# Half of a second matrix product in seven block products instead of eight, on one Trainium2 core

## The chip, the cores and the metric

The kernel runs on one core of one Trainium2 chip. The metric is the device time of one execution in microseconds; lower is better. Every run of the kernel before agrees with the others within 0.25%.

## What is computed

The inputs are 8 batches of 576 tokens, 8 heads of 64. A packed attention (32 packed queries a head) is followed by a mixer and a two-layer network with residual:

```
p_packed = sm_attn(p, k, v)                    # per head, 32 rows
x  = sm_attn(q, p_packed, p_packed)            # [B, 576, 8*64] after a transpose
h  = x^T @ U @ V                               # rank 32, along the tokens
u  = x + h^T
ch = relu(u @ w_ch1) @ w_ch2                   # 512 -> 2048 -> 512
out = u + ch
```

All of it is float32 in and out. The matrix products of the network run in fp32r with each operand split in a high and a low part, so that one product takes three passes (high x high, high x low, low x high).

## The kernel before

**Layout.** A batch has 576 = 9 x 64 tokens. Eight of the nine make four tiles of 128 tokens; the ninth, 64 tokens a batch, is called LAST. The hidden size 2048 is cut in 16 blocks `kt` of 128. The network's two products are called GEMM 1 (to hidden, L749) and GEMM 2 (back to 512 columns, L780).

**Opening.** A list of words (`opening`, L154) sets the order of everything up to batch 0: it loads and converts the weights, computes the packed attention of all batches, and runs attention and most of the network of batch 0. The weights of GEMM 2 stay in SBUF as `w2h` and `w2l` for the whole kernel, and w1 as four tiles `w1t`. For each batch w1 is multiplied by that batch's packed rows (`fold`, L536 to L560), which gives `wth` and `wtl`, the weights that GEMM 1 uses.

**Steady state.** From batch 1 on a loop (L923) runs, for each `kt`: GEMM 1 of this block (`gemm1`, 12 matmuls: 6 of 320 columns for row half 0, which holds the ninth tokens, and 6 of 256 for row half 1), one or two steps of the attention of the next batch (`steps`), and GEMM 2 of the block before (`gemm2`: four token tiles, three matmuls of 512 columns each, into four PSUM banks `o`). After a row half of GEMM 1 ScalarE writes relu as the high part `hh`, ScalarE keeps the ninth tokens in `hj`, and VectorE writes the low part `hl` straight from PSUM (L758 to L770). Every fourth block one `fold` follows. The residual u reaches `o` as small matmuls (`add_u`, L791) from tiles that `get` (L721) has brought back from HBM. At the end of a batch `store` (L797) copies the four banks out.

**Ninth tokens.** Two batches' LAST tokens make one tile of 128. After every second batch `joint` (L819) runs GEMM 2 for it, 48 matmuls of 512 columns, with parts split by `joint_parts` (L807), and `store_joint` (L835) writes it. The last batch's joint product is the program's last matmul work.

**What sets the order.** In the opening and in the loop the program's order is the order in which each engine gets its instructions; nothing is rescheduled. An engine that waits holds everything behind it. Nearly all DMAs are issued by SP's queue in program order.

Of the kernel before, what the change touches and what calls it, by code (L numbers as in the profile page):

```python
# [20 lines left out]
def packed_attention_mixer_kernel(  # L21
# [114 lines left out]
    w1t = [pipe.tile([P, DF], F32, name=f"w1t{x}", tag=f"w1t{x}") for x in range(4)]  # L136
# [191 lines left out]
    def attention(b, res):  # L328
# [92 lines left out]
        def put():  # L421
            for g in range(2):
                nc.sync.dma_start(out=aD[b][g * P:g * P + P], in_=st["aT", g])
            nc.sync.dma_start(out=ppD[b].rearrange("(g p) d -> p g d", g=2), in_=ppall[:, b])
# [20 lines left out]
        if b < 2:  # L445
# [90 lines left out]

    def fold_products(b, c):
        f_ps = [bank() for _ in range(2)]
        for h in range(H):
            g, z = h // 4, h % 2  # L540
            xs, zs = slice(32 * (h % 4 ^ g), 32 * (h % 4 ^ g) + 32), slice(64 * z, 64 * z + 64)
            nc.tensor.matmul(f_ps[g][xs], lhsT=ppT[b][zs, g, xs], rhs=w1t[h // 2][zs, QW * c:QW * c + QW],  # L542
                             start=True, stop=True)
        return f_ps
# [156 lines left out]
    def close_sA():  # L701
        actx.close()
        sB = pools["B"] = ctx.enter_context(tc.tile_pool(name="sB", bufs=2, reuse_waits="tile"))
        kept["hj"] = sB.tile([P, NK + 1, P], F32, name="hj", bufs=1)
        kept["aP"] = sB.tile([P, H, P], F32, name="aP", bufs=1)
# [9 lines left out]
    def jslot(b, kt):  # L715
        return NK if kt == 0 and (b // 2) % 2 else kt


    aL, ppP = {}, {}

    def get(b):  # L721
        sB, aP = pools["B"], kept["aP"]
        aL[b] = sB.tile([32, H, I], F32, name="aL", bufs=2)
        ppP[b] = sB.tile([P, H, D], F32, name="ppP", bufs=2)
        a, y = (x.rearrange("(h n) x -> n h x", n=32) for x in (aD[b], ppD[b]))
        for t in range(4):
            ts_ = slice(32 * t, 32 * t + 32)
            nc.sync.dma_start(out=aP[ts_], in_=a[:, :, cols(t)])
            nc.sync.dma_start(out=ppP[b][ts_], in_=y)
        nc.sync.dma_start(out=aL[b], in_=a[:, :, LAST])  # L730
# [10 lines left out]
    class Batch:  # L741
        def __init__(self, b):
            self.b = b
            self.ah, self.al = res[b]
            self.js = slice(I * (b % 2), I * (b % 2) + I)
            self.h, self.p = {}, {}
            self.o = None

        def half1(self, kt, r):  # L749
            c, kq = divmod(kt, 2)  # L750
            wh, wl = wt[self.b, c]
            ks, ns = slice(kq * P, kq * P + P), HALF[r]
            h_ps = self.p[kt, r] = psT.tile([P, 512], F32, name="h_ps", tag="k")
            for g in range(2):
                mm3(h_ps[:, :ns.stop - ns.start], (wh[:, g, ks], wl[:, g, ks]),
                    (self.ah[:, g, ns], self.al[:, g, ns]), g == 0, g == 1)

        def high1(self, kt, r):  # L758
            if kt not in self.h:
                self.h[kt] = tuple(pools["B"].tile([P, SM], F32R, name=f"h{x}", tag=f"h{x}", bufs=2) for x in "hl")  # L760
            nc.scalar.activation(self.h[kt][0][:, 4 * I * r:4 * I * r + 4 * I], self.p[kt, r][:, :4 * I], AF.Relu)  # L761

        def last1(self, kt):
            nc.scalar.activation(kept["hj"][:, jslot(self.b, kt), self.js], self.p[kt, 0][:, LAST], AF.Relu)  # L764
# [26 lines left out]
        def add_u(self):  # L791

            for h, t in product(range(H), range(4)):
                ts_ = slice(32 * t, 32 * t + 32)
                nc.tensor.matmul(self.o[t][:, place(h)], lhsT=kept["aP"][ts_, h], rhs=ppP[self.b][ts_, h], start=False, stop=False)  # L795

        def store(self):  # L797
            for j in range(2):
                os_ = bits_tile().bitcast(F32).rearrange("p x t -> p (x t)").rearrange("p (a x) -> p a x", a=2)
                nc.scalar.copy(os_[:, 0], self.o[2 * j])  # L800
                nc.vector.tensor_copy(os_[:, 1], self.o[2 * j + 1])
                for a in range(2):
                    c0 = j + 2 * a
                    nc.sync.dma_start(
                        out=out[self.b].rearrange("(i c) m -> i c m", c=NT)[:, c0:c0 + 5:4], in_=os_[:, a])

    def joint_parts(b, n):  # L807

        hi, lo = conv_tile(F32R), conv_tile(F32R)
        k0 = 4 * n  # L810
        for (dst, src) in ((slice(0, 1), jslot(b, k0)), (slice(1, 4), k0 + 1)):
            w = dst.stop - dst.start
            src = kept["hj"][:, src:src + w].rearrange("p k x -> p (k x)")
            cs = slice(P * dst.start, P * dst.stop)
            nc.scalar.copy(hi[:, cs], src)
            nc.vector.tensor_tensor(lo[:, cs], src, hi[:, cs].bitcast(F32), op=ALU.subtract)
        return hi, lo

    def joint(b, parts):  # L819

        oj = pools["O"].tile([P, DM], F32, name="o", tag="o")
        for kt in range(NK):
            if kt % 4 == 0:
                hi, lo = parts.pop(0)
                if kt // 4 + 2 < NK // 4:
                    parts.append(joint_parts(b, kt // 4 + 2))
            cs = slice(P * (kt % 4), P * (kt % 4) + P)
            mm3(oj, (hi[:, cs], lo[:, cs]), w2_parts(kt), kt == 0, kt == NK - 1)
            if kt == 0:
                for h, i in product(range(H), range(2)):  # L830
                    nc.tensor.matmul(oj[I * i:I * i + I, place(h)], lhsT=aL[b - 1 + i][:, h], rhs=ppP[b - 1 + i][:32, h],
                                     start=False, stop=False)
        return oj

    def store_joint(b, oj):  # L835
        os_ = conv_tile(F32)
        n = DM // 2
        nc.scalar.copy(os_[:, :n], oj[:, :n])
        nc.vector.tensor_copy(os_[:, n:], oj[:, n:])
        for i, queue in enumerate((nc.sync, nc.scalar)):  # L840
            queue.dma_start(out=out[b - 1 + i].rearrange("(i c) m -> c i m", c=NT)[8], in_=os_[I * i:I * i + I])
# [80 lines left out]
    last, parts = kept["cur"], []  # L922
    for b in range(1, B):  # L923
        now = Batch(b)
        oj = None
        ahead = attention(b + 2, res) if b + 2 < B else []
        for kt in range(NK):
            now.gemm1(kt)
            if oj and kt == 1:
                store_joint(b - 1, oj)  # L930
            if steps and (b < 2 or kt % 4 != 2) and (b, kt) != (1, 0):
                steps.pop(0)()
            if kt > 0:
                now.gemm2(kt - 1)
            else:
                last.gemm2(NK - 1)
                last.store()
                if last.b % 2 == 1:
                    oj = joint(last.b, parts)
            if kt % 4 == 2 and (b, kt) != (B - 1, NK - 2):  # L940
                n = b * NPC + kt // 4 + 1
                fold(n // NPC, n % NPC)
            if kt == 6:
# [47 lines left out]
```

## Time and profile before

| | |
|---|---|
| median of 3 runs | 805.23 us (804.2 to 806.06) |
| profiled execution | 805.29 us |
| its span in the profile | 803.5 us |
| mean granted TensorE clock | 0.998 |
| HBM read, written | 53.64 MB, 15.60 MB |
| DMA queue of SP | 27.6% of 16 engines' time |

The difference of 1.8 us between the execution and its span lies outside of what the profiler shows. The page cuts the span in 40 slices of 20.1 us; a digit is the busy share in tenths:

```profile
PE   8999999999999999999999999999999999999997
DVE  4898789843443234333334233333434233332231
ACT  4788645543233232333234232333234232332221
PEclk9999999999999999999999999999999999999999
DMA  9999984460004200230012200230022200030001
```

PE is TensorE, DVE VectorE, ACT ScalarE, POOL GpSimd; "PEld" in other views is TensorE's weight load, which overlaps the matmuls. The opening takes the first eight slices, where VectorE and ScalarE are busy too. Behind it only TensorE is full.

### The profile page before, as it was taken

Reading aid. Unit: us, or ns where it says so; the run is one execution under the profiler, and the core shown is the slowest. Engines: PE = TensorE matmul, PEld = TensorE weight load, DVE = VectorE, ACT = ScalarE, POOL = GpSimd, SP = SyncE. Lnnn points to the kernel's source line nnn. Section 1 sums busy time; section 2 is a strip of 40 time slices with the busy share of each in tenths; the row PEclk is TensorE's granted clock in tenths of the full one; section 3 lists DMA queues with packets and bytes.
Section 4 is the critical chain, followed back from the end, with each engine's and each line's share of the span. In section 5 each row is a group of like instructions: output and inputs, shape, how many; then the busy total and the mean of one; then the engine's idle time right before and its main releaser. Section 6 shows DMA issues by size and latency. Waiting matters only on the chain.

```text
span 803.5 us, 15400 instructions
## 1 busy us (share of the span) xinstructions
PE 790.7 (98%) x6272; PEld 640.6 (80%) x6272; DVE 361.1 (45%) x797; ACT 307.7 (38%) x879; POOL 79.3 (10%) x109
## 2 busy tenths in 40 slices
PE   8999999999999999999999999999999999999997
PEld 6667778788888788878888788888887788878886
DVE  4898789843443234333334233333434233332231
ACT  4788645543233232333234232333234232332221
POOL 1023021101110011101100011101100011100000
PEclk9999999999999999999999999999999999999999
DMA  9999984460004200230012200230022200030001
GB/s 323 335 354 296 302 195 138 131 195 1 1 1 151 57 1 2 81 113 2 1 66 86 56 1 2 81 114 1 1 66 86 56 2 1 16 113 1 1 1 65
DMA packets 59285, 70.22 MB, mean 87 GB/s; under 512 B 20816, under 2 KB 40272, under 8 KB 59216
## 3 DMA queue, kind: packets, MB, share of 16 engines
q1 hardware_dynamic: 58896, 68.73, 27.6%
q8 instruction: 49, 0.80, 0.4%
q10 hardware_dynamic: 320, 0.52, 0.2%
q14 instruction: 20, 0.16, 0.1%
HBM read 53.64 MB, written 15.60 MB: 86 GB/s over the span
## 4 chain that ended last, share of the span: by engine, by line
PE 88%; DMA 4%; DVE 4%; ACT 3%; issue 1%; POOL 0%; SPq 0%; ACTq 0%; DVEq 0%
PE o L95 16%; PE o L97 16%; PE o L96 16%; PE h_ps L95 9%; PE h_ps L97 8%; PE h_ps L96 8%; PE t_ps L542 4%; DMA bits<-in_moe_w_ch_dram 3%; PE o L795 2%; PE t_ps L297 1%; DMA kx<-in_k_dram 1%; PE t_ps L317 1%; PE t_ps L323 1%; PE t_ps L408 1%; PE m_ps L669 1%
## 5 line engine op out<-in xcount | busy, mean ns | idle before, releaser
L95 PE MATMUL o<-w2h,hh 128*128 128x512 f32 x512 | 205.0, 400 | 0.0
L97 PE MATMUL o<-w2h,hl 128*128 128x512 f32 x512 | 201.9, 394 | 0.3 <-DVE hl L769 0.3
L96 PE MATMUL o<-w2l,hh 128*128 128x512 f32 x512 | 201.2, 393 | 0.0
L769 DVE SCALAR_TENSOR_TENSOR hl<-h_ps,hh 128x256 fp32r<-128x256 f32 x256 | 106.4, 422 | 197.3 <-ACT hj L764 179.5
L761 ACT ACTIVATE hh<-h_ps 128x256 fp32r<-128x256 f32 x256 | 98.4, 386 | 180.7 <-PE h_ps L97 168.9
L95 PE MATMUL h_ps<-ah,wth 128*128 128x320 f32 (+1 forms) x512 | 158.0, 309 | 0.2 <-ACT hj L764 0.2
L96 PE MATMUL h_ps<-al,wth 128*128 128x320 f32 (+1 forms) x512 | 150.8, 295 | 0.0
L97 PE MATMUL h_ps<-ah,wtl 128*128 128x320 f32 (+1 forms) x512 | 150.7, 294 | 0.0
L95 PEld LDWEIGHTS h_ps<-ah,wth 128*128 128x128 f32 x512 | 96.3, 188 | 25.9 <-issue 20.2
L97 PEld LDWEIGHTS o<-w2h,hl 128*128 128x128 f32 x512 | 96.2, 188 | 22.4 <-DVE hl L769 0.7
L95 PEld LDWEIGHTS o<-w2h,hh 128*128 128x128 f32 x512 | 96.5, 189 | 21.1 <-issue 4.9
L96 PEld LDWEIGHTS o<-w2l,hh 128*128 128x128 f32 x512 | 96.5, 188 | 16.4
L96 PEld LDWEIGHTS h_ps<-al,wth 128*128 128x128 f32 x512 | 96.3, 188 | 2.2
L97 PEld LDWEIGHTS h_ps<-ah,wtl 128*128 128x128 f32 x512 | 96.6, 189 | 0.0
L555 DVE TENSOR_TENSOR wtl<-t_ps,wth 128x256 fp32r<-128x256 f32 x128 | 48.5, 418 | 95.0 <-ACT wth L553 92.0
L553 ACT CAST wth<-t_ps 128x256 fp32r<-128x256 f32 x128 | 43.4, 375 | 100.5 <-PE t_ps L542 94.0
L440 POOL TENSOR_TENSOR al<-aT,ah 128x320 fp32r<-128x320 f32 (+1 forms) x32 | 27.6, 866 | 223.9 <-ACT ah L436 195.8
L364 POOL TENSOR_TENSOR e<-e,m 128x576 f32<-128x576 f32 x16 | 19.0, 1186 | 272.7 <-DVE m L360 272.7
L542 PE MATMUL t_ps<-w1t,ppT 64*32 64x512 f32 x512 | 34.8, 601 | 0.0
L306 ACT COPY xT<-t_ps 128x512 f32<-128x512 f32 x30 | 17.6, 586 | 38.8 <-PE t_ps L297 38.1
L764 ACT ACTIVATE hj<-h_ps 128x64 f32<-128x64 f32 x128 | 28.2, 220 | 2.0 <-PE h_ps L97 1.1
L364 POOL TENSOR_TENSOR e<-e,s 128x576 f32<-128x576 f32 x16 | 19.3, 1207 | 93.7 <-DVE s L376 77.9
(125 smaller groups left out, 806.0 us busy)
## 6 DMA issues: line engine op xcount, KB each, us to landing
bits<-in_moe_w_ch_dram SPq DMA_DIRECT2D x32, 512.0 KB, 4.5
kx<-in_k_dram SPq DMA_DIRECT2D x16, 576.0 KB, 6.3
x<-in_q_dram SPq DMA_DIRECT2D x16, 576.0 KB, 5.0
vt<-in_v_dram SPq DMA_DIRECT2D x32, 256.0 KB, 6.0
out_dram<-bits SPq DMA_DIRECT2D x32, 256.0 KB, 2.4
aD<-aT SPq DMA_DIRECT2D x16, 288.0 KB, 2.2
aP<-aD SPq DMA_DIRECT2D x32, 128.0 KB, 3.3
ppP<-ppD SPq DMA_DIRECT2D x32, 64.0 KB, 3.0
```

Of the source, the lines that this page charges most:

```text
L95: nc.tensor.matmul(ps, lhsT=lh, rhs=rh, start=start, stop=False)
L96: nc.tensor.matmul(ps, lhsT=lh, rhs=rl, start=False, stop=False)
L97: nc.tensor.matmul(ps, lhsT=ll, rhs=rh, start=False, stop=stop)
L306: copy(scalar)(t[:, 2 * h:2 * h + 2, :4 * I].rearrange("p z (k y) -> p z k y", k=2), src)
L364: nc.gpsimd.tensor_tensor(e, e, st[what, g].unsqueeze(2).to_broadcast([P, S // 32, 32]), op=op)
L440: nc.gpsimd.tensor_tensor(al[:, g, ns], aT[:, ns], ah[:, g, ns].bitcast(F32), op=ALU.subtract)
L542: nc.tensor.matmul(f_ps[g][xs], lhsT=ppT[b][zs, g, xs], rhs=w1t[h // 2][zs, QW * c:QW * c + QW], start=True, stop=True)
L553: nc.scalar.copy(hi[:, g], src)
L555: nc.vector.tensor_tensor(lo[:, g], src, hi[:, g].bitcast(F32), op=ALU.subtract)
L761: nc.scalar.activation(self.h[kt][0][:, 4 * I * r:4 * I * r + 4 * I], self.p[kt, r][:, :4 * I], AF.Relu)
L764: nc.scalar.activation(kept["hj"][:, jslot(self.b, kt), self.js], self.p[kt, 0][:, LAST], AF.Relu)
L769: nc.vector.scalar_tensor_tensor(hl[:, ms], self.p[kt, r][:, :4 * I], 0.0, hh[:, ms].bitcast(F32), op0=ALU.max, op1=ALU.subtract)
```

## The change

Batches 0 and 1 run as before. From batch 2 on GEMM 2 is done differently.

**Sweeps.** A batch's 512 tokens are taken in two sweeps of 256 tokens (2 x 128), r = 0 and 1. A sweep goes over the hidden size in 8 pairs of blocks, c = 0 to 7. With the two token tiles, the two hidden blocks of a pair and the two halves of 256 output columns, a pair is a 2 x 2 by 2 x 2 block product. For even c (`PAIRS`) it is made by Strassen's method in Winograd's form: 7 block products of three 256-column matmuls. For odd c the plain 8 block products are made. All of them accumulate in four PSUM banks per sweep (8 half banks, 7 of them Strassen terms), which are combined once, at the end of the sweep.

**Ninth tokens.** The LAST tokens of four batches (256 rows) make one more sweep after batches 3 and 7, in place of a joint product after each second batch. `save_last` writes each batch's ninth tokens to HBM (`hjD`).

**Operands.** VectorE makes the sums of the weights once, in the last blocks of batch 1 (`begin_sums`, `make_sums`, `split_sums`); they go over three of the four `w1t` tiles, so w1 is kept in HBM (`w1D`) and brought back in pieces of 1 MB (`stream_w1`) ahead of each fold. The sums of the activations are made per pair (`sums`, VectorE), and high and low parts are split from SBUF (`split_high` ScalarE, `split_low` VectorE), no longer from PSUM. GEMM 1 of row half 1 is computed in sweep 0 for c < 5 and its result written to HBM (`hold_out`, `hD`), and read back in sweep 1 (`load`).

**Order.** The loop of batches 2 to 7 is replaced by lists of words, as in the opening: `prologue`, `batch_steps` and, where a joint sweep follows, `joint_steps`.

```diff
+    def begin_sums(c):
...
+        nc.vector.tensor_tensor(x.rearrange("p (k n) -> p k n", k=2), h, l, op=ALU.add)
...
+    def make_sums(c):
...
+        vec(t[:, 0:2], x[:, 0:4:3], x[:, 1:2].to_broadcast([P, 2, HW_]), op=ALU.subtract)
+        vec(t[:, 2], t[:, 0], x[:, 3], op=ALU.add)
+        vec(t[:, 3], x[:, 2], t[:, 2], op=ALU.subtract)
...
+    def split_sums(c):
...
+        parts = [(h1, l1)] + [(room[:, i, 0], room[:, i, 1]) for room in rooms]
+        for k, (h, l) in enumerate(parts):
+            nc.scalar.copy(h, t[:, k])
+            nc.vector.tensor_tensor(l, t[:, k], h.bitcast(F32), op=ALU.subtract)
...
+    def stream_w1(c):
+        t = w1t["s"] = pipe.tile([P, 4, QW], F32, name="w1s", tag=f"w1t{NPC - 1}", bufs=1)
+        nc.sync.dma_start(out=t.rearrange("p x n -> p (x n)"), in_=w1D[c])
...
+    class Sweep:
+        def load(self, c):
+            src = hD[self.now.b][P * c:P * c + P] if self.r else hjD[self.q].rearrange("p (c x) -> p c x", c=8)[:, c]
+            l = self.l[c] = sums_tile()
+            nc.sync.dma_start(out=l[:, :4].rearrange("p k n -> p (k n)"), in_=src)
...
+        def leave(self, c, i):
...
+            nc.scalar.activation(dst[:, 256 * (i % 2):256 * (i % 2) + 256], src, AF.Relu)
...
+        def sums(self, c):
+            l, vec = self.l[c], nc.vector.tensor_tensor
+            vec(l[:, 4:6], l[:, 1:3], l[:, 0:1].to_broadcast([P, 2, P]), op=ALU.add)
+            vec(l[:, 6], l[:, 2], l[:, 4], op=ALU.add)
+            vec(l[:, 7], l[:, 3], l[:, 6], op=ALU.add)
+        def split_high(self, c):
+            t = pools["B"].tile([P, 2, 2 * SM], F32R, name="h", bufs=2)
+            h, lo = self.h[c] = tuple(t[:, z].rearrange("p (k n) -> p k n", n=P) for z in range(2))
+            ks = slice(1, 8) if c in PAIRS else slice(0, 4)
+            nc.scalar.copy(h[:, ks], self.l[c][:, ks])
+        def split_low(self, c):
...
+            nc.vector.tensor_tensor(lo[:, ks], self.l[c][:, ks], h[:, ks].bitcast(F32), op=ALU.subtract)
+        def add(self, x, z, lhs, rhs, last):
+            ps = self.o[x][:, HW_ * z:HW_ * z + HW_]
+            (lh, ll), (rh, rl) = lhs, rhs
+            for i, (a, b) in enumerate(((lh, rh), (lh, rl), (ll, rh))):
+                nc.tensor.matmul(ps, lhsT=a, rhs=b, start=x not in self.begun, stop=last and i == 2)
...
+        def products(self, c, x):
...
+            if c in PAIRS:
+                t3, t2, t4 = sums_of[c]
+                todo = (((0, 3, b21), (1, 1, b11)), ((0, 7, b22), (1, 5, b12)), ((0, 2, t4), (1, 4, t3)), ((1, 6, t2),))[x]
+            else:
+                t, y = 1 - x // 2, x % 2
+                todo = ((0, t, (b11, b12)[y]), (0, 2 + t, (b21, b22)[y]))
...
+        def empty(self, x, scalar):
+            m = self.m[x] = conv_tile(F32)
+            copy(scalar)(m, self.o[x])
+        def combine(self, k):
+            to, a, b, op = ((0, 0, 1, "add"), (31, 1, 31, "subtract"), (1, 31, 11, "add"), (1, 10, 1, "add"),
+                            (21, 31, 21, "add"), (11, 21, 11, "add"), (20, 20, 21, "subtract"), (21, 30, 11, "subtract"))[k]
...
+            nc.vector.tensor_tensor(to, a, b, op=getattr(ALU, op))
...
-    for b in range(1, B):
...
-                now.gemm2(kt - 1)
+    batch_steps = (
+        "N H H E N C N G L L N E N q0 O D H q0av H E U G G H G F0 C G S E D E G W L F1 F1 H F2 F1 F1 F2 F2 H F2 q2 q1 "
...
+            run(joint_steps, "" if b < B - 1 else "n")
+    run(" ".join(8 * ["N"] + 2 * ["O"]))
```

In the word lists H is one row half of GEMM 1 for one block, E its relu, U, C and D are `sums`, `split_high` and `split_low`, G is `products`, M is `empty`, N `combine`, O the store, and R, Rj and RJ are `load`; F0 to F2 are the fold and its split, and words in small letters the attention of the next batch. A word that ends in n belongs to the batch after, and v puts a copy on VectorE.

**First place: TensorE within a batch.** Before, GEMM 1's last matmul of a block and the start of GEMM 2 (`o` from `w2h`, `w2l` and the split activations `hh`, `hl`):

```order
L97 MATMUL h_ps<-ah,wtl 128x256
L95 MATMUL o<-w2h_108,hh 128x512
L96 MATMUL o<-w2l_109,hh 128x512
L97 MATMUL o<-w2h_108,hl 128x512
L95 MATMUL o<-w2h_108,hh 128x512
```

Now, in the middle of a Strassen pair (`ws` are the sums of the weights, `h` the split sums of the activations, `t_ps<-w1s,ppT` a fold):

```order
L944 MATMUL o<-w2h_118,h 128x256
L944 MATMUL o<-ws_3315,h 128x256 x3
L944 MATMUL o<-ws_3313,h 128x256 x3
L95 MATMUL h_ps<-ah,wth 128x320
L96 MATMUL h_ps<-al,wth 128x320
L97 MATMUL h_ps<-ah,wtl 128x320
L95 MATMUL h_ps<-ah,wth 128x320
L96 MATMUL h_ps<-al,wth 128x320
L97 MATMUL h_ps<-ah,wtl 128x320
L944 MATMUL o<-ws_3314,h 128x256 x3
L557 MATMUL t_ps<-w1s,ppT 32x512 x8
L944 MATMUL o<-w2h_118,h 128x256
```

GEMM 2 has moved from 512 to 256 columns a matmul, every matmul still has its own weight load, and it stands in shorter runs between GEMM 1, folds and attention.

**Second place: VectorE towards the end of an attention half.** Before, the second half's softmax sum (`s`), the low parts of two blocks, the transposes of the attention and a fold's low parts:

```order
L376 RECIPROCAL s<-s 128x18
L769 SCALAR_TENSOR_TENSOR hl<-h_ps,hh 128x256 x2
L380 STREAM_TRANSPOSE aT_7625<-e 128x576
L401 TENSOR_TENSOR x<-t_ps,x 128x512
L769 SCALAR_TENSOR_TENSOR hl<-h_ps,hh 128x256 x2
L555 TENSOR_TENSOR wtl<-t_ps,wth 128x256 x4
```

Now the same stretch, at the change from sweep 0 to sweep 1 (`bits` hold the activations and their sums, `os` take the copied banks):

```order
L382 RECIPROCAL s<-s 128x18
L938 TENSOR_TENSOR h<-bits,h 128x512
L925 TENSOR_TENSOR bits<-bits 128x256
L926 TENSOR_TENSOR bits<-bits 128x128
L927 TENSOR_TENSOR bits<-bits 128x128
L386 STREAM_TRANSPOSE aT_4253<-e 128x576
L938 TENSOR_TENSOR h<-bits,h 128x896
L982 COPY os<-o 128x512 x2
L938 TENSOR_TENSOR h<-bits,h 128x512
L407 TENSOR_TENSOR x<-t_ps,x 128x512
```

The low parts read from PSUM are gone; the last split of sweep 0, the sums and the split of sweep 1's first pair and two bank copies stand around the attention's transpose.

**Third place: the end of VectorE's program.** Before, the copies of the last batch, the split of the last joint parts and the copy of half a bank:

```order
L801 COPY bits<-o 128x512 x2
L816 TENSOR_TENSOR os<-hj,os 128x128
L816 TENSOR_TENSOR os<-hj,os 128x384
L816 TENSOR_TENSOR os<-hj,os 128x128
L816 TENSOR_TENSOR os<-hj,os 128x384
L839 COPY os<-o 128x256
```

Now, the end of the second joint sweep:

```order
L927 TENSOR_TENSOR bits<-bits 128x128
L938 TENSOR_TENSOR h<-bits,h 128x896
L988 TENSOR_TENSOR os<-os 128x256 x2
L938 TENSOR_TENSOR h<-bits,h 128x512
L982 COPY os<-o 128x512 x2
L988 TENSOR_TENSOR os<-os 128x256 x8
```

Eight combinations now stand behind the last product, where one copy of 256 columns stood.

344 lines of the change are left out of this document (245 added, 99 removed), and 10 rows, old and new, of tables (batch_steps, joint_steps).

## The prediction

> **What bounds the kernel now.** I read the page's first part, then the busy time by stages, to see whether TensorE's 98% holds where the change works.
>
> ```profile
> PE 790.7 (98%) x6272; PEld 640.6 (80%) x6272; DVE 361.1 (45%) x797; ACT 307.7 (38%) x879; POOL 79.3 (10%) x109
> ```
>
> The stages (from : to, length, then each engine's busy time and count):
>
> ```profile
> core 0: us, PE busy (x) PEld busy (x) DVE busy (x) ACT busy (x) POOL busy (x), PEclk, DMA share, GB/s
> 220.00:250.00 30.00, 29.90 (x194) 24.66 (x193) 11.47 (x28) 11.53 (x36) 3.23 (x4) 1.00 0.20 67
> 251.00:798.50 547.50, 546.49 (x3772) 450.49 (x3771) 190.55 (x441) 169.83 (x505) 42.07 (x50) 1.00 0.13 41
> 330.00:690.00 360.00, 359.20 (x2510) 294.97 (x2509) 132.61 (x305) 117.36 (x346) 33.66 (x40) 1.00 0.15 46
> ```
>
> From batch 2's start (about 251 us) to the last matmul TensorE has work in 546.5 of 547.5 us, at a granted clock of 1.00. Time goes there only if TensorE gets less to do, and comes back wherever it is made to wait. VectorE has 37% of 330 to 690, ScalarE 33%. Busy times of matmuls overlap, so their price is the distance of starts. From the timeline, the first and last such pairs from 251 us on:
>
> ```profile
> 251.81 0.31 PE L95 MATMUL h_ps<-ah,wth 128*128 128x320 f32 x1
> ...
> 252.69 0.28 PE L95 MATMUL h_ps<-ah,wth 128*128 128x256 f32 x1
> 252.80 0.28 PE L96 MATMUL h_ps<-al,wth 128*128 128x256 f32 x1
> ...
> 254.05 0.39 PE L96 MATMUL o<-w2l,hh 128*128 128x512 f32 x1
> 254.27 0.40 PE L97 MATMUL o<-w2h,hl 128*128 128x512 f32 x1
> ...
> 780.82 0.28 PE L96 MATMUL h_ps<-al,wth 128*128 128x256 f32 x1
> 780.93 0.28 PE L97 MATMUL h_ps<-ah,wtl 128*128 128x256 f32 x1
> ...
> 798.49 0.39 PE L96 MATMUL o<-w2l,os 128*128 128x512 f32 x1
> 798.71 0.40 PE L97 MATMUL o<-w2h,os 128*128 128x512 f32 x1
> ```
>
> Over the 480 gaps between 256-column matmuls of GEMM 1 the mean is 0.1169 us; over the 804 gaps behind the second and third passes of 512 columns it is 0.2310. Six matmuls of 320 columns take 0.88 (252.69 - 251.81), so 0.147 each. Two narrow matmuls thus cost 0.2338, 0.003 more than a wide one.
>
> **The change part by part.** *GEMM 2.* Removed from batch 2 on: 6 batches x 4 tiles x 16 blocks x 3 = 1152 wide matmuls, and 4 joint products x 48 = 192; in all 1344 x 0.2310 = 310.5 us. Added: a sweep has 4 even pairs of 7 products and 4 odd ones of 8, three matmuls each, so 180; 12 sweeps and 2 of ninth tokens give 2520 narrow ones, x 0.1169 = 294.6 us. TensorE gains **15.9 us**. The eighth saved on half of the work would be 19.4 (168 x 0.1155); the split in narrow matmuls takes 3.5 of it back. GEMM 1, folds, attention and residual matmuls keep their numbers and forms.
>
> Against that price speaks a rule, weighed here beside the rows. The Trainium skill, "TensorE: Matmul & The Clock Gate", section Back-to-back issue gap, says that in a stream of weight loads and matmuls both set the spacing, 81 ns at 128 columns and 131 at 512. A straight line gives an estimate of 98 ns at 256 columns, and the exchange would cost 70 us more (2520 x 98 - 1344 x 131 ns). The section's isolated gap, columns / 2.4 + 2.5 ns, would give 109.2 and 215.8 and a gain of 15.0 us. The trace has 116.9 and 231.0, and loads at every narrow matmul: it sides with the second form, in its fixed part too (2.8 ns by my two means).
>
> *VectorE and ScalarE in a sweep.* The new shapes are not all in the trace; the nearest operations are these (mean ns of one behind the bar):
>
> ```profile
> L816 DVE TENSOR_TENSOR os<-hj,os 128x384 fp32r<-128x384 f32 x16 | 8.9, 553 | 0.9
> L816 DVE TENSOR_TENSOR os<-hj,os 128x128 fp32r<-128x128 f32 x16 | 5.5, 342 | 22.5 <-ACT os L815 22.5
> L769 DVE SCALAR_TENSOR_TENSOR hl<-h_ps,hh 128x256 fp32r<-128x256 f32 x256 | 106.4, 422 | 197.3 <-ACT hj L764 179.5
> L801 DVE COPY bits<-o 128x512 f32<-128x512 f32 x16 | 11.1, 691 | 13.6 <-PE o L97 13.6
> ```
>
> ```profile
> L815 ACT CAST os<-hj 128x384 fp32r<-128x384 f32 x16 | 8.2, 513 | 0.0
> L815 ACT CAST os<-hj 128x128 fp32r<-128x128 f32 x16 | 4.8, 300 | 23.8 <-PE o L96 23.8
> L800 ACT COPY bits<-o 128x512 f32<-128x512 f32 x16 | 9.4, 587 | 9.6 <-PE o L97 9.0
> ```
>
> L816 rises by 0.824 ns an element (211 / 256): 0.45 us for 256, 0.66 for 512, 0.98 for 896 (an estimate beyond the rows). L815 rises by 0.832: 0.62 for 512, 0.94 for 896. So `sums` cost 0.45 + 2 x 0.34 = 1.13, `split_low` 0.98 or 0.66, `combine` 8 x 0.45; a sweep's VectorE work is 4 x 1.13 + 4 x 0.98 + 4 x 0.66 + 3.6 = 14.7 us. A batch gains two of them and a quarter of a joint sweep (33.0), and loses 32 low parts of 0.422 (13.5) and half a joint split (1.8): +17.7 us. The 547.5 us from 251 on hold six batches, 91 us each, and lose 15.9 / 6 = 2.7. VectorE's 31.8 us of a batch (190.55 / 6) becomes 49.5 of about 88.6, 56%; ScalarE's 28.3 grows by 2.25 sweeps of 4 x (0.94 + 0.62), less 1.6 for half a joint split, to 40.7, 46%. As a total both hide behind TensorE; what decides is the order.
>
> *The change of sweep.* All four banks must be emptied before they are used again, while the attention's second softmax runs on VectorE, GpSimd and ScalarE (GpSimd's row is the first of these):
>
> ```profile
> L364 POOL TENSOR_TENSOR e<-e,m 128x576 f32<-128x576 f32 x16 | 19.0, 1186 | 272.7 <-DVE m L360 272.7
> ...
> L367 ACT ACTIVATE e<-e 128x576 f32<-128x576 f32 x16 | 10.9, 684 | 2.8 <-POOL e L364 2.7
> ...
> L360 DVE TENSOR_REDUCE m<-e 128x18 f32<-128x576 f32 x16 | 12.0, 749 | 0.3
> L372 DVE TENSOR_REDUCE s<-e 128x18 f32<-128x576 f32 x16 | 11.9, 746 | 0.9 <-ACT e L367 0.3
> L380 DVE STREAM_TRANSPOSE aT<-e 128x576 f32<-128x576 f32 x16 | 12.4, 773 | 7.6 <-POOL e L364 7.5
> ```
>
> Queued on VectorE between the second scores and sweep 1's first product: a split (0.98), two score transposes (about 0.9), the maximum 0.75, then GpSimd 1.19 and ScalarE 0.68, the total and its two small steps (about 1.2), a split 0.66, sums 1.13, the transpose 0.77, a split 0.98: 9.2 us. TensorE has the residual (about 1), a GEMM 1 half (0.88), 69 narrow products (8.1) and eight transposes (about 0.8): 10.8. The slack of 1.5 us must pay some ten hand-offs, which the tail below shows at about 0.04 each. Behind the split wait two bank copies on VectorE (0.69 each), and for them the next products. I take 0.1 us a sweep, **1.5 us** in all; the ends are 0 and the 1.7 (0.98 + 0.69) of a sweep whose cover is gone, x 14 = 23.
>
> *Batch 1's end.* The weight sums put on VectorE, for four pairs, an addition of 1024 elements (1.08), 0.66 + 2 x 0.45, and 4 x 0.45: 17.7 us in the stage 220 to 250, where it has 11.5 of 30 now. 29.2 of 30 fits just so; cost 0, at most some 3. Then the second 1 MB piece of w1 is asked for when the fold ahead of it has ended, with one GEMM 1 (6 x 0.147 + 6 x 0.117) and one GEMM 2 (12 x 0.231) left to hide it, 4.35 us:
>
> ```profile
> bits<-in_moe_w_ch_dram SPq DMA_DIRECT2D x32, 512.0 KB, 4.5
> x<-in_q_dram SPq DMA_DIRECT2D x16, 576.0 KB, 5.0
> out_dram<-bits SPq DMA_DIRECT2D x32, 256.0 KB, 2.4
> ```
>
> Twice a row of half the size is 9.0, the row itself 4.5; I take 5.4, nearer to the row, so **1.0 us** of wait (0.2 to 4.7). Later pieces have 7 us and more.
>
> *The last joint sweep* has no GEMM 1, fold or attention between its products. A pair of pairs is 45 x 0.117 = 5.3 us of TensorE; the buffer of an even pair needs a load (256 KB: 2.4, up to 5.0 by the larger row), sums 1.13, 0.94 and 0.98: 5.5 to 8.0. Three rounds: 0.6 to 8 us late. I take **1.2**, near the row of its own size.
>
> *The tail.* Before, from the last matmul to the end:
>
> ```profile
> 799.15 0.37 ACT L838 COPY os<-o 128x256 f32<-128x256 f32 x1 [5.03 <-PE o L97]
> 799.55 0.43 DVE L839 COPY os<-o 128x256 f32<-128x256 f32 x1 [4.84 <-ACT os L838]
> 800.00 0.50 SPq L841 DMA_DIRECT2D out_dram<-os  x1
> ```
>
> From 798.71 to 803.5, 4.8 us, with 0.85 between the matmul's end and the issue. Now one bank copy (0.59), seven combinations (7 x 0.45 = 3.15; the eighth can go ahead) and a second issue (0.5) stand there: 4.2, so **+3.3 us**.
>
> Sum: -15.9 + 1.5 + 1.0 + 1.2 + 3.3 = -8.9. The profiled span 803.5 becomes 794.6; with the 1.8 us outside of it 796.4, and as that execution (805.29) lies 0.06 over the median, **796.5 us**.
>
> **The rivals.** *Clean order.* No wait but the tail: 805.2 - 15.9 + 3.3 = 792.6; if a run of narrow matmuls also has no fixed part (0.1155 each), 789. For it: TensorE waits 1 us in 547 now. Against: the chains above have 1.5 us to spare at best.
>
> *The change of sweep becomes the bound.* A fixed order gives back each miss, since TensorE takes no other work. It decides from (15.9 - 5.5) / 14 = 0.74 us a sweep: from there the kernel is **slower**; with the cover gone, 1.7 us a sweep, 805.2 - 15.9 + 5.5 + 23 = 818. For it: L364 and L372 stand in one chain through three engines. Against: VectorE's 56% leave it time to catch up within a sweep.
>
> *Weight loads set the pace.* Each is this long:
>
> ```profile
> L97 PEld LDWEIGHTS h_ps<-ah,wtl 128*128 128x128 f32 x512 | 96.6, 189 | 0.0
> ```
>
> If loads of 189 ns could not overlap each other, 2520 would take 476 us and the kernel 805.2 + 476 - 310.5 + 5.5, or about 976. Against: GEMM 1 has these loads at 117 ns a matmul today, though in runs of six. The 98 ns of the skill's first form, put in place of both prices, would mean 882.
>
> That the seven products are not made can be left out: the listed program has 180 matmuls a sweep.
>
> **How the numbers follow.** Forecast 60%, for itself 793 to 802; clean order 16%; change of sweep 22%, of which 9% end within 0.2% of before and 13% slower; loads 2%. A measurement of this kernel can tell some 0.2% (1.6 us) from no change. Faster 0.76, same 0.09, slower 0.15. The range 790 to 808 leaves out the lower part of the clean order (5%), the worst of the slow one (11%) and the loads.
>
> **What would show it.** Right: narrow `o` matmuls 0.117 apart; TensorE without a gap over 0.5 us within batches 2 to 6; a gap of about 1 us ahead of batch 2's second fold; gaps of a microsecond in all in the last joint sweep; 8 us from the last matmul to the end. Wrong: `o` matmuls 0.12 or more apart in long runs (2.5 us for each ns), gaps at every change of sweep on VectorE's `h` (split) or `os` (copy), or VectorE over 70% busy within a batch.

## The result and the profile after

| | before | changed |
|---|---|---|
| median of 4 runs each | 805.64 us | 796.72 us |
| ratio, 95% interval | | 0.9888 [0.9868, 0.9908] |
| span of the profiled execution | 803.5 | 795.3 |
| batch 2's first fold to the last matmul | 246.30 to 798.71: 552.4 | 246.84 to 787.54: 540.7 |
| last matmul to the end of the span | 4.8 | 7.7 |

The changed kernel is 1.1% faster, and 0.2 us from the 796.5 forecast. That the sum fits does not say that its terms do. The engines' totals of the changed kernel first:

```profile
PE 776.3 (98%) x7448; PEld 688.2 (87%) x7448; DVE 491.6 (62%) x1009; ACT 380.0 (48%) x987; POOL 80.6 (10%) x109
```

Its stages, for comparison with those of the prediction (length, then busy time and count of each engine):

```profile
core 0: us, PE busy (x) PEld busy (x) DVE busy (x) ACT busy (x) POOL busy (x), PEclk, DMA share, GB/s
220.00:250.00 30.00, 29.58 (x187) 23.85 (x186) 24.96 (x52) 13.55 (x43) 4.53 (x4) 1.00 0.18 61
252.00:787.00 535.00, 530.97 (x4942) 497.27 (x4941) 302.93 (x620) 239.10 (x604) 41.87 (x50) 1.00 0.43 131
330.00:690.00 360.00, 359.22 (x3359) 334.89 (x3357) 210.92 (x435) 166.03 (x424) 36.49 (x44) 1.00 0.43 132
```

Between 330 and 690 TensorE is as full as before, though VectorE has risen from 37% to 59% and ScalarE from 33% to 46%: there the exchange of matmuls came through whole. Waits of TensorE from 250 us on stand in three places (by line, what it waited for: us in total, times, longest):

```profile
PE o L944 <- DVE h L938: 3.1, 2, 2.3
PE t_ps L557 <- DMA w1s<-w1D: 1.0, 1, 1.0
```

The long one lies in the last joint sweep. SP's queue, VectorE and TensorE there, from three timelines of the changed kernel:

```profile
757.38 3.48 SPq L906 DMA_DIRECT2D bits<-hjD  x2
760.90 0.42 SPq L884 DMA_DIRECT2D aP<-aD  x1
```

```profile
764.50 0.42 DVE L925 TENSOR_TENSOR bits<-bits 128x256 f32<-128x256 f32 x1 [2.54 <-DMA bits<-hjD]
...
765.50 0.68 DVE L938 TENSOR_TENSOR h<-bits,h 128x512 fp32r<-128x512 f32 x1
```

```profile
763.66 0.28 PE L944 MATMUL o<-w2l,h 128*128 128x256 f32 x1
766.24 0.80 PE L944 MATMUL o<-w2h,h 128*128 128x256 f32 x2 [2.30 <-DVE h L938]
766.83 0.41 PE L944 MATMUL o<-w2l,h 128*128 128x256 f32 x1
```

The second of the two loads in the first row (it is for the joint sweep's third pair) waited on SP's queue for a buffer until 760.5, when VectorE had ended the low split of the first pair (L938, 759.41 to 760.50), and landed at 764.4. VectorE's next instruction needs it (L925), and the low split of the second pair (765.50), whose data had long been there (ScalarE's high part was done at 761.9), stands behind. TensorE needed that split at 763.8. The wait has an echo; windows of 2 us, the granted clock third from the end:

```profile
764.00:766.00 2.00, 0.00 (x0) 0.00 (x0) 1.43 (x4) 0.25 (x1) 0.00 (x0) 1.00 0.81 145
766.00:768.00 2.00, 1.76 (x8) 1.76 (x9) 1.47 (x3) 0.69 (x1) 0.00 (x0) 0.54 0.39 86
768.00:770.00 2.00, 2.00 (x13) 2.00 (x13) 0.48 (x2) 0.00 (x0) 0.00 (x0) 0.61 0.49 169
770.00:772.00 2.00, 2.00 (x19) 2.00 (x19) 0.72 (x2) 0.62 (x1) 0.00 (x0) 1.00 0.06 19
```

Behind 2.30 us of idleness the clock is about half for 3.4 us; the first two matmuls start 0.38 apart and then 14 of them 0.21 instead of 0.117. That is 1.6 us more (0.26 and 14 x 0.095). The wait itself makes the next matmul 2.46 late (2.58 from start to start instead of 0.117), so it costs 4.1 in all.

The end of the changed kernel, where one copy of 256 columns stood before:

```profile
787.54 0.28 PE L944 MATMUL o<-w2h,h 128*128 128x256 f32 x1
787.76 0.42 DVE L988 TENSOR_TENSOR os<-os 128x256 f32<-128x256 f32 x1
787.86 0.58 ACT L982 COPY os<-o 128x512 f32<-128x512 f32 x1 [1.55 <-DVE os L982]
788.47 2.94 DVE L988 TENSOR_TENSOR os<-os 128x256 f32<-128x256 f32 x7 [0.30 <-ACT os L982]
789.88 2.66 SPq L997 DMA_DIRECT2D out_dram<-os  x4
```

One combination beside the last copy and seven behind it (2.94 us), and stores that are issued as the halves are ready.

### The profile page after: what moved, and what is told of

It reads as the page before. It is cut to its first block, busy times and chain, and to the rows that moved or that the text cites. A ratio compares the mean times of both kernels' runs of the same rounds, so it can differ in the third digit from the quotient of the medians.

```text
span 795.3 us, 18421 instructions
## 1 busy us (share of the span) xinstructions
PE 776.3 (98%) x7448; PEld 688.2 (87%) x7448; DVE 491.6 (62%) x1009; ACT 380.0 (48%) x987; POOL 80.6 (10%) x109
## 4 chain that ended last, share of the span: by engine, by line
PE 86%; DVE 5%; DMA 4%; ACT 3%; issue 1%; POOL 0%; SPq 0%; ACTq 0%; DVEq 0%; POOLq 0%
PE o L944 37%; PE h_ps L95 9%; PE h_ps L96 8%; PE h_ps L97 8%; PE t_ps L557 4%; PE o L95 3%; PE o L97 3%; PE o L96 3%; DMA bits<-in_moe_w_ch_dram 2%; PE o L970 2%; PE t_ps L303 2%; PE t_ps L323 1%; PE t_ps L414 1%; PE m_ps L683 1%; PE s_ps L323 1%
## 5 line engine op out<-in xcount | busy, mean ns | idle before, releaser
L944 PE MATMUL o<-w2h,h 128*128 128x256 f32 x1344 | 265.0, 283 | 3.1 <-DVE h L938 3.1
L944 PEld LDWEIGHTS o<-w2h,h 128*128 128x128 f32 x1344 | 216.9, 189 | 8.5 <-issue 5.0
L944 PE MATMUL o<-w2l,h 128*128 128x256 f32 x672 | 188.7, 281 | 0.0
L95 PE MATMUL h_ps<-ah,wth 128*128 128x256 f32 (+1 forms) x512 | 156.7, 306 | 0.6 <-DVE h L782 0.4
L938 DVE TENSOR_TENSOR h<-bits,h 128x896 fp32r<-128x896 f32 x112 | 104.1, 929 | 84.2 <-ACT h L933 84.2
L933 ACT CAST h<-bits 128x896 fp32r<-128x896 f32 x112 | 87.5, 781 | 132.7 <-PE o L944 90.2
L96 PE MATMUL h_ps<-al,wth 128*128 128x256 f32 (+1 forms) x512 | 150.7, 294 | 0.0
L97 PE MATMUL h_ps<-ah,wtl 128*128 128x256 f32 (+1 forms) x512 | 150.5, 294 | 0.0
L944 PEld LDWEIGHTS o<-w2l,h 128*128 128x128 f32 x672 | 127.2, 189 | 0.0
L918 ACT ACTIVATE bits<-h_ps 128x256 f32<-128x256 f32 x132 | 49.9, 384 | 39.1 <-PE h_ps L97 27.9
L95 PE MATMUL o<-w2h,h 128*128 128x512 f32 x128 | 52.0, 406 | 0.0
L97 PE MATMUL o<-w2h,h 128*128 128x512 f32 x128 | 50.6, 395 | 0.1
L370 POOL TENSOR_TENSOR e<-e,m 128x576 f32<-128x576 f32 x16 | 19.0, 1185 | 303.1 <-DVE m L366 303.1
L447 POOL TENSOR_TENSOR al<-aT,ah 128x320 fp32r<-128x320 f32 (+1 forms) x32 | 28.5, 907 | 201.5 <-ACT ah L443 173.4
```

The lines of the kernel that those rows point to most:

```text
L95: nc.tensor.matmul(ps, lhsT=lh, rhs=rh, start=start, stop=False)
L96: nc.tensor.matmul(ps, lhsT=lh, rhs=rl, start=False, stop=False)
L97: nc.tensor.matmul(ps, lhsT=ll, rhs=rh, start=False, stop=stop)
L370: nc.gpsimd.tensor_tensor(e, e, st[what, g].unsqueeze(2).to_broadcast([P, S // 32, 32]), op=op)
L447: nc.gpsimd.tensor_tensor(al[:, g, ns], aT[:, ns], ah[:, g, ns].bitcast(F32), op=ALU.subtract)
L918: nc.scalar.activation(dst[:, 256 * (i % 2):256 * (i % 2) + 256], src, AF.Relu)
```

## The experiments

Up to batch 2's first fold all variants of the changed kernel run the same program (eight_products alone leaves out the weight sums there, as do the two kernels without sweeps), but in the profiled executions that fold began anywhere from 245.3 to 248.4 us. So the stretch from that fold to the last matmul, and the tail behind it, are compared beside the medians (all in us; the medians of before were 804.2 to 804.7 beside these runs):

| kernel | median | fold to last matmul | tail |
|---|---|---|---|
| before | 805.64 | 552.4 | 4.8 |
| changed | 796.72 | 540.7 | 7.7 |
| eight_products | 807.94 | 555.3 | 4.5 |
| before_narrow | 813.29 | 559.7 | 4.7 |
| split_twice | 802.28 | 546.0 | 7.7 |
| split_thrice | 811.19 | 554.0 | 7.7 |
| thrice_unscaled | 807.39 | 550.2 | 7.7 |
| order_moved | 795.70 | 538.1 | 7.7 |
| more_rooms | 793.70 | 536.7 | 7.7 |
| early_sums | 794.66 | 539.2 | 5.2 |
| all_three | 791.76 | 536.3 | 5.2 |
| sums_behind | 789.10 | 535.4 | 5.0 |

### What are seven products worth?

```diff
-    PAIRS = (0, 2, 4, 6)
+    PAIRS = ()
...
-            m = self.m[x] = conv_tile(F32)
-            copy(scalar)(m, self.o[x])
+            if x % 2 == 0:
+                self.m[x] = conv_tile(F32)
+            y = HW_ * (x % 2)
+            copy(scalar)(self.m[x - x % 2][:, y:y + HW_], self.o[x][:, :HW_])
...
         def combine(self, k):
+            return
```

> Sweeps, parked halves and joint sweeps as in the changed kernel, but every pair with the plain 8 products: no sums of weights or activations, no combinations, 4 blocks split instead of 7, half banks copied. If the seven products give what their matmuls cost: +168 narrow matmuls x 0.1173 us = +19.7, and back come the two waits of the joint sweeps (0.94 and 4.2), the longer tail (3.0) and the weight sums of batch 1 (about 1.1): 796.7 + 19.7 - 9.2 = about 807. If instead VectorE's work in the sweeps paced TensorE, taking it away would return much of the 19.7: 800 or less, and gaps of TensorE within batches 2 to 6 that the changed kernel has and this one has not.

Measured 807.94 (1.0041 of before [1.0026, 1.0056]). Seven products instead of eight bring 10 to 12 us (807.94 - 796.72 = 11.2 by the medians; 1.5%, or 12, by the two ratios; 9.9 by the two profiled spans, 805.2 and 795.3); without them the sweeps make the kernel slower than before. Of TensorE's waits only the fold's is left:

```profile
PE t_ps L557 <- DMA w1s<-w1D: 0.7, 1, 0.7
```

VectorE's busy time falls from 491.6 to 350.7, and no wait of TensorE within the sweeps of the batches goes with it, since there was none: VectorE did not pace these sweeps. From batch 1's third fold to batch 2's first this kernel needs 43.3 us, the kernel before 43.3, the changed one 44.3: the weight sums, which are not made here, cost 1.1.

### What does a narrow matmul cost in GEMM 2?

```diff
+    def mm3_halves(ps, lhs, rhs, start, stop):
+        for y in range(2):
+            cs = slice(DM // 2 * y, DM // 2 * y + DM // 2)
+            mm3(ps[:, cs], lhs, tuple(r[:, cs] for r in rhs), start and y == 0, stop and y == 1)
...
-            mm3(self.o[t], (hh[:, ts_], hl[:, ts_]), w2_parts(kt), kt == 0, kt == NK - 1)
+            if self.b < 2:
+                mm3(self.o[t], (hh[:, ts_], hl[:, ts_]), w2_parts(kt), kt == 0, kt == NK - 1)
+            else:
+                mm3_halves(self.o[t], (hh[:, ts_], hl[:, ts_]), w2_parts(kt), kt == 0, kt == NK - 1)
```

> The kernel before, with each 512-column matmul of GEMM 2 from batch 2 on (and of the joint products) made as two of 256 columns, 1344 becoming 2688. If a narrow matmul costs 0.1173 us in long runs, as the trace of the changed kernel has it: 1344 x (2 x 0.1173 - 0.2310) = +4.8, about 810.4. If 256 columns cost clearly more where runs are long or the weight loads cannot keep up, each ns is 2.7 us: at 0.125 us it would be 831; by the Trainium skill's straight line between 81 and 131 ns an estimate of +87 us.

Measured 813.29 (1.0112 [1.0095, 1.0129]), 8.6 over before; the stretch 7.3. One run of 24 narrow matmuls of GEMM 2 in this kernel, its first, its last, and the matmul behind it:

```profile
759.94 0.28 PE L95 MATMUL o<-w2h,hh 128*128 128x256 f32 x1
...
762.67 0.28 PE L97 MATMUL o<-w2h,hl 128*128 128x256 f32 x1
762.79 0.31 PE L95 MATMUL h_ps<-ah,wth 128*128 128x320 f32 x1
```

(762.79 - 759.94) / 24 = 0.1188. Over its 2560 undisturbed gaps of this kind the mean is 0.1182, and 1344 x (2 x 0.1182 - 0.2310) = 7.3 is the whole of the stretch's growth. The changed kernel has 0.1173 (2331 gaps), the one with eight products 0.1179; the same matmul in GEMM 1 0.1169. The split in halves costs twice what the row of GEMM 1 gave (1344 x 0.0028 = 3.8), and what makes the last ns was not tried. The straight line between the two sustained figures of the Trainium skill ("TensorE: Matmul & The Clock Gate", section Back-to-back issue gap), an estimate of +87 us, is far off for these matmuls.

### How much slack has the change of sweep?

```diff
-            nc.vector.tensor_tensor(lo[:, ks], self.l[c][:, ks], h[:, ks].bitcast(F32), op=ALU.subtract)
+            for _ in range(2 if c == 0 else 1):
+                nc.vector.tensor_tensor(lo[:, ks], self.l[c][:, ks], h[:, ks].bitcast(F32), op=ALU.subtract)
```

In split_thrice the 2 of this edit is a 3.

> The changed kernel, with the low split of each sweep's first pair (128x896 on VectorE, 1.09 us) done twice, 14 times in all. If the change of sweep has the 1.5 us of slack that the prediction counted: nothing in the 12 sweeps of the batches; the joint sweeps, whose third load waits for this split, lose 1 to 2 us in all: 798 to 799. If there is no slack: 14 x 1.09 = +15, 812.

> The same split three times, 2.18 us more in each sweep. With 1.5 us of slack, 12 x 0.7 = 8 us in the batches and 2 to 4 in the joint sweeps: 807 to 809, with gaps of about 0.7 us at each change of sweep. With more slack than counted: the joint sweeps alone, 799 to 801. Without slack: 14 x 2.18, 827.

Measured 802.28 and 811.19, more than 1.5 us of slack would give. TensorE's wait for the split, twice and then three times:

```profile
PE o L945 <- DVE h L939: 4.4, 9, 2.3
```

```profile
PE o L945 <- DVE h L939: 13.7, 10, 2.4
```

With 2.18 us added TensorE starts its next matmul 1.59 after the one before at the change to sweep 1 of each of the six batches, 1.47 late; with 1.09 added, 0.34 late. The slack is 0.7 to 0.75. The change to the next batch's sweep 0 showed no wait even with 2.18. What had eaten the other half of the counted 1.5 stands at 302 us of the changed kernel, GpSimd first, then VectorE:

```profile
302.81 1.16 POOL L370 TENSOR_TENSOR e<-e,s 128x576 f32<-128x576 f32 x1 [2.16 <-DVE s L382]
```

```profile
302.95 1.56 DVE L938 TENSOR_TENSOR h<-bits,h 128x512 fp32r<-128x512 f32 x1 [0.28 <-ACT h L933]
```

This split takes 0.68 to 0.69 where GpSimd is idle. So, on top of the split done three times:

```diff
         def each(g, what, op):
+            if what == "s" and b > 2:
+                return
```

> The kernel with the split done three times, and GpSimd's multiplication with the inverse softmax sum (e<-e,s) left out for batches 3 to 7, so that these rows of attention stay unnormalised. In the changed kernel the 128x512 split of sweep 0's last pair takes 1.56 us where it runs beside that GpSimd operation, and 0.69 elsewhere. If GpSimd holds VectorE up: the split takes 0.69 everywhere, and the five waits of 1.47 us at the change to sweep 1 in batches 2 to 6 become about 0.6: 811.2 - 4.4 = about 807. If the 1.56 us have another cause (their place, the operands' landing): they stay, and the time stays at 811.

Measured 807.39, 3.8 less than with the multiplication. The group of these splits by form and TensorE's wait, with GpSimd's operation and without it:

```profile
L939 DVE TENSOR_TENSOR h<-bits,h 128x512 fp32r<-128x512 f32 x52 | 40.1, 771 | 14.8 <-ACT h L933 14.8
```

```profile
L941 DVE TENSOR_TENSOR h<-bits,h 128x512 fp32r<-128x512 f32 x52 | 35.7, 687 | 14.3 <-ACT h L935 14.2
...
PE o L947 <- DVE h L941: 9.5, 10, 2.6
```

In batches 2 to 6 the next matmul now starts 0.73 behind the last, 0.61 late instead of 1.47. In batch 7, which has no attention beside it, 1.61 stayed: there GpSimd takes nothing, but TensorE also lacks the attention's transposes as cover. Without GpSimd the slack in batches 2 to 6 is 2.18 - 0.61 = 1.57: the 1.5 that the prediction counted.

### Order, buffers, and the end

Two words moved; then loads of the last joint sweep into w1's free tile; then the combinations ahead of the last pair:

```diff
-        "F0n XG Sn Hn a0 Hn Ln En F1n F1n Hn F2n Ln En XMv XG En U XG XMv C Hn Hn D En Wn Hn En XO XMv Ln F1n Hn XO "
+        "XG Hn F0n Sn a0 Hn Ln En F1n F1n Hn F2n Ln En XMv XG En U XG XMv C Hn Hn D En Wn Hn En XO XMv Ln F1n Hn XO "
...
-        "ZJ Hn G Ln G C F0n G U F1n G D C RJ G F1n D G N G RJ N G G Hn G C G D G U RJ G G N C N G D G RJ G O G C Sn G "
+        "ZJ Hn G Ln G C F0n G F1n G D U C RJ G F1n D G N G RJ N G G Hn G C G D G U RJ G G N C N G D G RJ G O G C Sn G "
```

> Two words moved. In the joint sweeps the sums of the third pair (which wait for its load) now stand behind the low split of the second pair on VectorE, not ahead of it; and batch 2's second fold stands behind one GEMM 2 tile and one GEMM 1 half. If the order on VectorE makes the two waits of 0.94 and 2.46 us: the first goes, the second shrinks to about 1.5 us, since the load itself (landing at 764.5) is late for the third pair, and TensorE keeps full clock there (another 1.5): -0.9 - 2.5, and -1.1 for the fold; about 792. If the load alone makes the wait: the gaps move one pair on and stay as long, and only the fold's 1.1 goes: 795.6.

Measured 795.70, and less than expected: the first joint sweep's wait did not move. Three waits are left on the split, 1.8 us in all:

```profile
PE o L944 <- DVE h L938: 1.8, 3, 0.8
```

The two in the last joint sweep (0.6 and 0.7 late, where 1.5 was expected) leave the clock at 1.00. The fold no longer waits for w1; the GEMM 2 tile that now stands ahead of it waits 0.4 for its low part instead. The stretch is 2.6 shorter, the median only 1.0: this profiled execution was already 0.9 later at the first fold.

```diff
-            l = self.l[c] = sums_tile()
+            if self.q == 1 and c % 4 < 2:
+                if c == 0:
+                    t = pipe.tile([P, 4, QW], F32, name="hjs", tag=f"w1t{NPC - 1}", bufs=1)
+                    kept["hjs"] = t.rearrange("p x n -> p (x n)").rearrange("p (s k n) -> p s k n", s=2, k=8)
+                l = self.l[c] = kept["hjs"][:, c % 4]
+            else:
+                l = self.l[c] = sums_tile()
```

> In the last joint sweep alone, pairs 0, 1, 4 and 5 are loaded into the tile of w1, which is free by then, so four buffers take turns instead of two and the third pair's load no longer waits for the first pair's split. If that buffer is the cause of the 2.46 us wait: no gap over 0.3 us in the last joint sweep, a granted clock of 1.00 throughout it, -4.2 us: 792.5. If the load is late for another reason (the residual's eight small DMAs on the same queue, or hjD written late): the gap stays.

Measured 793.70, the stretch 3.9 shorter. In the last joint sweep TensorE has no wait, and its clock stays at 1.00, in windows of 4 us:

```profile
764.00:768.00 4.00, 4.00 (x37) 4.00 (x36) 2.10 (x4) 1.56 (x2) 0.00 (x0) 1.00 0.31 89
768.00:772.00 4.00, 4.00 (x37) 4.00 (x36) 3.46 (x7) 0.94 (x1) 0.00 (x0) 1.00 0.22 72
```

The eight residual DMAs are issued as before: two more buffers were enough.

In the edit for the tail the word `O` (the store) moves forward in `joint_steps` too, and the eight `N` and two `O` at the end of the program go:

```diff
+            if self.q == 1:
+                x, z = 2 * (1 - z) + x // 2, x % 2
...
+            if self.q == 1 and (c, x) == (6, 3):
+                self.early()
+            if self.q == 1 and c == 7 and x % 2:
+                self.final(x // 2)
...
+        def early(self):
...
+            vec(m[3][:, lo], m[1][:, lo], self.o[1][:, hi], op=ALU.subtract)
+            vec(m[1][:, hi], m[3][:, lo], m[3][:, hi], op=ALU.add)
+            vec(m[2][:, lo], m[3][:, lo], self.o[1][:, lo], op=ALU.add)
+            vec(m[2][:, hi], m[2][:, lo], m[3][:, hi], op=ALU.add)
+
+        def final(self, k):
+            nc.vector.tensor_tensor(self.m[2 * k], self.o[2 + k], self.m[1 + k], op=(ALU.add, ALU.subtract)[k])
+            self.put(1 - k)
```

> In the last joint sweep the Strassen halves of the banks are kept apart from the plain ones, copied and combined on ScalarE and VectorE while the last, plain pair is multiplied; behind the last product stand one 512-column addition from PSUM and its stores. If the combinations make the longer tail: from the last matmul to the end 5.2 us instead of 7.8, -2.6: 794.1. If the end is set by the issue and landing of the last stores instead: 7 us or more remain.

Measured 794.66, and the tail is 5.2 as expected:

```profile
786.89 0.28 PE L946 MATMUL o<-w2h,h 128*128 128x256 f32 x1
787.21 0.69 DVE L981 TENSOR_TENSOR os<-o,os 128x512 f32<-128x512 f32 x1 [0.34 <-PE o L946]
```

In the last joint sweep the wait was 1.6 us here, and the clock did not fall behind it. A new one of 0.8 stands behind the first joint sweep, where GEMM 1 waits for a relu of ScalarE (L918); it is in split_twice too, and its cause is open.

> The three edits together; they lie at different places, so their gains should add: -0.9 in the first joint sweep, -1.1 at the fold, -4.2 in the last joint sweep, -2.6 in the tail: 796.7 - 8.8 = about 788. If the waits only move to the next hand-off: 792 or more.

Measured 791.76 (0.9849 [0.9834, 0.9863]), almost 4 us over the 788 expected. The stretch lost 4.3 where 6.2 was expected, and the tail 2.6; the first joint sweep's wait of 0.8 still stood, and in the profiled execution the first fold began 1.5 later than in the changed kernel's. At the end of a batch VectorE has the next sums (`U`) ahead of the split of sweep 1's last pair (`D`), so that one word was moved:

```diff
-        "y2 Hn E y3 Hn Ln C En G Ln En F0n G F1n F2n G N Hn U O Hn En pu D Rj Hn En F1n Wn F1n Hn F2n Ln En Hn En F1n "
+        "y2 Hn E y3 Hn Ln C En G Ln En F0n G F1n F2n G N Hn O Hn En pu D U Rj Hn En F1n Wn F1n Hn F2n Ln En Hn En F1n "
```

> The kernel with the three edits together, and one more word moved: at the end of each batch the next sums (128x256 and two 128x128 additions) stand behind the low split of sweep 1's last pair, not ahead of it. If the order on VectorE makes the wait of 0.94 us ahead of the first joint sweep: it goes, 791.8 - 0.9 = about 791. If the wait comes from GpSimd's operation beside it, whichever of the two comes first: half of it stays; if the sums are then late themselves, gaps of the same size appear behind the joint sweep's first products.

Measured 789.10 (0.9815 [0.9800, 0.9831]), the best of these kernels, and faster than the kernel before and the changed one. The stretch fell by 0.9 and that wait is gone; the rest of the 2.7 between the two medians lies, in the two profiled executions, ahead of batch 2's first fold (248.4 and 246.2 us), where the programs are the same. It is not the word's, and its cause is open.

The order was enough to remove the wait, but it was not alone in making it. In the changed kernel VectorE lost about as much to GpSimd just ahead of it:

```profile
413.48 2.45 POOL L447 TENSOR_TENSOR al<-aT,ah 128x320 fp32r<-128x320 f32 x3 [1.32 <-ACT ah L443]
```

```profile
414.41 0.92 DVE L988 TENSOR_TENSOR os<-os 128x256 f32<-128x256 f32 x1
415.26 0.96 DVE L925 TENSOR_TENSOR bits<-bits 128x256 f32<-128x256 f32 x1
```

Both take 0.42 where GpSimd is idle, so 1.04 us went here, and TensorE's next matmul came 0.94 late. Whether the wait goes with GpSimd's operation alone was not tried. The kernel with the word moved, its steady part and its last joint sweep:

```profile
250.00:781.00 531.00, 530.56 (x4947) 496.54 (x4946) 304.82 (x627) 240.23 (x609) 41.86 (x50) 1.00 0.44 133
763.00:781.00 18.00, 18.00 (x208) 17.80 (x207) 11.79 (x25) 4.39 (x7) 0.00 (x0) 1.00 0.20 61
```

## Why the prediction was right

The forecast held in its time and its main mechanism: the exchange of matmuls came through at about its price, and within the batches the other engines stayed hidden behind it. That the time is right to 0.2 us is luck: four terms were off by 1 to 3 us and cancelled. Each against the profiled executions:

| term | predicted | measured |
|---|---|---|
| 1344 wide for 2520 narrow matmuls | -15.9 | -14.9 |
| other matmuls of the stretch | 0 | -2.9 |
| weight sums in batch 1 | 0 | +1.1 |
| second piece of w1 | +1.0 | +1.1 |
| changes of sweep | +1.5 | +0.9 |
| last joint sweep | +1.2 | +4.1 |
| tail | +3.3 | +2.9 |
| opening | 0 | -0.5 |
| sum | -8.9 | -8.2 |

- *The exchange.* The price from GEMM 1 was 0.4 ns too low: 2520 x 0.1173 = 295.6 for 310.5. The before_narrow and eight_products runs show the two sides of it. The split in halves alone costs 7.3 at the 0.1182 of that run. The 168 matmuls that seven products save are 19.7 at 0.1173, of which 11.2 reach the median: the weight sums (1.1), the waits of the joint sweeps (5.0) and the longer tail (3.2), which eight_products does not have, make up the rest within 1 us. The rival of weight loads setting the pace is out: loads of 0.19 us stood at every matmul of 0.117.
- *Other matmuls.* The -2.9 is what is left of the stretch's -11.7 when the other rows are taken off. It is absent where only the width changed (before_narrow), and -4.3 with the new order and eight products. The prediction had these matmuls keep their price because they keep their forms, and the traces show that the price hangs on the neighbours. From the first fold on the new order changes between matmuls of the two GEMMs and all others (folds, scores, transposes, residual) 175 times instead of 215, and the starts at a change are late, here at a fold of the changed kernel:

```profile
281.09 0.28 PE L97 MATMUL h_ps<-ah,wtl 128*128 128x256 f32 x1
281.30 1.09 PE L557 MATMUL t_ps<-w1s,ppT 64*32 64x512 f32 x16
282.31 0.39 PE L95 MATMUL h_ps<-ah,wth 128*128 128x256 f32 x1
282.54 0.28 PE L96 MATMUL h_ps<-al,wth 128*128 128x256 f32 x1
282.65 0.29 PE L97 MATMUL h_ps<-ah,wtl 128*128 128x256 f32 x1
```

The gap ahead of the fold is 0.21 and the one behind the first GEMM matmul 0.23, both 0.117 in a run. Over all changes these two gaps exceed those of a run by 14.0 us before and 13.9 in before_narrow, by 10.0 in the changed kernel (its wait for w1 left off) and 9.9 with eight products. So some 4 us went there, against the 2.9 that the table has left over. What went the other way, and what makes a change cost time, was not tested by itself.

- *Weight sums.* "29.2 of 30 fits just so" did not quite: VectorE has 24.96 of 30, and yet TensorE lost 1.1, within the bound of 3. It lies in two places: batch 1's last fold (at 225 us) takes 1.69 us instead of 1.02, and at 241.6 us GEMM 1 starts some 0.6 late, waiting for a low part of VectorE. The share of a stage did not show such late results.
- *Change of sweep.* In the plain sweeps no wait appeared: the slack was there, but 0.7 and not 1.5. The step that failed is the chain's second split "0.66", which takes 1.56 beside GpSimd. split_thrice is the rival of slower sweeps made real, 1.0092 of before: it takes 2.18 us more on VectorE at each change of sweep to get there. The one wait of 0.9 stood ahead of the first joint sweep; moving one word on VectorE removed it (sums_behind), though GpSimd had its part in it.
- *Last joint sweep.* The mechanism was named: the buffer of an even pair waits for its load and sums. But 1.2 was taken near the small end, and two things were not seen: a split whose data was ready queued behind the late sums, and the clock that falls when TensorE idles. more_rooms took both away with the buffers alone.
- *Tail.* Right, by its own steps: the bank copy took 0.58 for 0.59, the seven combinations 2.94 for 3.15. (The prediction's 0.85 in the kernel before runs from the copy's start at 799.15; from the matmul's end, 799.11, it is 0.89, which changes little.) early_sums took 2.6 of the 2.9 back.

## What to carry to other kernels

Where one engine is full, an exchange of its work comes through at the price of its start-to-start gaps, if each of the other engines' results comes in time one by one; a stage's busy share cannot show that, the order of one queue around each hand-off can, as far as no other engine makes one of the operations longer. Look for instructions that are ready but stand behind one that waits for a load, and give the last stage, where no other work covers a load, more buffers. A sum that comes out right should still be checked term by term: four terms here were off by 1 to 3 us each.

## What the hardware showed beside this

**GpSimd holds VectorE, by the operands' place.** In the kernel before, the low parts were read from PSUM, and all took the same time, GpSimd or not (180 operations, ns min/median/max). In the changed kernel the sums, whose inputs are both in SBUF, reach 1.14 us where they run beside L370. The fold's low part, still from PSUM, never stood beside L370, but ten times beside another operation of GpSimd, L447, and kept its 0.41 to 0.42; the sum and the combination that stood beside L447 at 414 to 416 us took 0.96 and 0.92 instead of 0.42:

```profile
L769 DVE SCALAR_TENSOR_TENSOR hl<-h_ps,hh x180: 411/424/426, 270.9 to 758.7; 128x256 fp32r<-128x256 f32 x180
```

```profile
L926 DVE TENSOR_TENSOR bits<-bits x53: 291/292/1139, 258.7 to 756.1; 128x128 f32<-128x128 f32 x53
```

```profile
L569 DVE TENSOR_TENSOR wtl<-t_ps,wth x92: 412/418/426, 257.3 to 714.4; 128x256 fp32r<-128x256 f32 x92
```

The Trainium skill, "SBUF — State Buffer", section "SBUF: two separate sides", has this as a lock: a VectorE operation with two SBUF inputs and a GpSimd operation that reads SBUF share one pair of ports, and the later one waits for the whole instruction. The trace agrees (0.29 becomes 1.14, 0.69 becomes 1.56). A change that moves an operand from PSUM to SBUF can take on this wait.

**The clock falls after less than 3.4 us.** The Trainium skill, "TensorE: Matmul & The Clock Gate", section "What's actually happening", gives half clock after an idle window of about 3.4 us. Here less was enough: 2.30 us of waiting in the changed kernel, and 2.3, 2.4 and 2.6 in split_twice, split_thrice and thrice_unscaled; 1.6 us (early_sums) was not, nor were the waits of 1.3 in split_thrice. Half clock then lasted some 3.4 us. It need not begin when the work does: in thrice_unscaled TensorE works again from 775.9 us on, and the clock, third from the end, falls more than 1 us later:

```profile
774.00:776.00 2.00, 0.06 (x1) 0.06 (x1) 1.68 (x4) 0.78 (x1) 0.00 (x0) 1.00 0.66 144
776.00:778.00 2.00, 2.00 (x15) 2.00 (x16) 1.76 (x3) 0.16 (x1) 0.00 (x0) 0.84 0.43 122
778.00:780.00 2.00, 2.00 (x11) 2.00 (x11) 0.00 (x0) 0.11 (x1) 0.00 (x0) 0.50 0.51 151
```

Nor does every execution seem to pay for it: of the changed kernel's four, two had a mean granted clock of 0.995 (797.06 and 797.24 us), two of 0.998 and 0.997 (796.38 and 795.42). Only one of them, at 0.995, was profiled.
